# A table of task order for one Trainium2 core, rewritten up to the second chunk's first gate product

## The chip, the core and the metric

The kernel runs on one core of one Trainium2 chip. The time is the device time of one execution in microseconds. Three runs of the kernel before gave 203.19, 204.13 and 204.41 us, median 204.13 us. A run is called faster or slower than another here when they differ by more than a measurement of this kernel can tell from no change, about 1%.

## What is computed

A transformer block on x of 2048 tokens by 512, in bf16, with six modulation vectors worked out from a condition c. Its first half is a linear attention whose feature map has two softmaxes per head (32 heads of 16); its second half is a gated feed-forward of 1376 columns.

```python
mod = (silu(c) @ w_mod)                       # sa, ca, ga, sb, cb, gb
h = layernorm(x) * (1 + ca) + sa
q, k, v = split(h @ wqkv)
phi_q = concat(softmax(q @ w_phi), softmax(-(q @ w_phi)))
phi_k = concat(softmax(k @ w_phi), softmax(-(k @ w_phi)))
kv = sum over tokens of phi_k (x) v;  z = sum over tokens of phi_k
o = (phi_q @ kv) / (phi_q @ z + 1e-6)
x = x + ga * (o @ wo)
h = layernorm(x) * (1 + cb) + sb
x = x + gb * ((sigmoid(h @ w_gate) * (h @ w_up)) @ w_down)
```

## The kernel before

The 2048 tokens are 16 tiles of 128. All weights stay in SBUF. The kernel has two halves with a barrier between them, since kv needs every token's key: the keys and values of all 16 tiles first, then numerators, output product, second normalisation and feed-forward by chunks of 1, 1, 2, 4, 4 and 4 tiles (`CHUNKS`).

Each piece of work is a task with a name, a tuple of engines that can do it, and the data that it reads and writes. The names used below, with N a tile or group number:

- `ld_...`: a load, issued on SP. `warm0`, `warm1_N`: matmuls on zeros. `tpw`, `wTc`, `fold`, `foldc`: the key (1) and query (0) weights are transposed and multiplied with w_phi once, on PE, and copied out of PSUM on ACT.
- `modc1.0`, `modc1.1`, `modc1c0`, `modc1c1`: the first scale and shift, two halves, on PE and then ACT or DVE.
- `st1`, `rs1`, `nmr1`, `xn1`, `tph` or `xT1`, `hm1`: the first normalisation (statistics on DVE L702 and L703, root on ACT or POOL, mean times root on DVE L718, the normalised tile on ACT, POOL or DVE), its transposition on PE (L744) or by DMA, and the modulation into h1T (L751 on ACT, L753 on DVE and POOL).
- `K`, `e`, `n`, `r`, `phi`: key product (PE L817), two exponentials (ACT L776), their sums (DVE L780), reciprocals (DVE L798, or ACT L794 and L795) and the map (POOL or DVE L787). `V` and `va`: value product (PE L821) and its copy (ACT L836). `kv`: the sum over tokens in PSUM (PE L282); `kvn`, `kvz`: its masked copy kvb (DVE L294, L299).
- `Q`, `qe`, `qn`, `qphi`, `pT`: the same for queries (PE L871, ACT L776, DVE L780, POOL or DVE L784, two halves), and the map's transposition by DMA (SP L874).
- `num`, `rd`, `u`, `oT`, `out`: numerators (PE L326), reciprocal (DVE L329), quotient o (DVE L333), its transposition on PE or by DMA (SP L350), output product a_ps (PE L356).
- `x1`, `st2`, `rs2`, `nmr2`, `xn2`, `xnT`, `mod`: first residual sum (DVE L361), statistics, nmr (DVE L383), xn (ACT L400), transposition on PE (L415) or by DMA, modulation.
- `gK.F`, `tg`, `uK.F`, `hm`, `y`, `fin`: gate and up products of chunk K (PE L447), tanh (ACT L457), their product (DVE L468), down product (PE L485), last sum. `wo`, `wd`: the output and down weights times ga and gb (POOL L851, L860).

The order of all 1230 tasks is written out as one text, `ORDER`: one word per task, with a letter behind an @ where it isn't the task's first engine. Every engine works through its own tasks strictly in that order. `arrange` also hands out the buffers by it: a buffer's slot goes to the next task that needs one of its class once the last user stands in the list, so the order decides which earlier task a later one has to wait for. There are 8 PSUM banks, 7 buffers for maps and exponentials, and 10 for transposed query maps.

```python
for word in text.split():
    name, _, e = word.partition("@")
    t = self.tasks[name]
    t.eng = LETTER[e] if e else next(iter(t.alts))
    for b in t.bufs:
        if b.slot is None:
            b.slot = slots[b.cls].pop(0)
```

Of the kernel before, what the change touches and what calls it, by code (L numbers as in the profile page):

```python
# [43 lines left out]
hm1_00@A tph02 hm1_23 rs1_6@P hm1_13@A hm1_02 nmr1_3 st1_9 st1_8 xn1_5 tph03 K0a tph41 hm1_03@A tph40 xn1_4 K2a hm1_22@A hm1_12@A hm1_41@A hm1_40 wqT1 nmr1_6
ld_x3a st1_15 fold01 foldc01 tph42 K2b hm1_42@A K0b K3b e0.0 ld_wv0 tph32 tph30 tph31 wqT3 tph33 rs1_5@P nmr1_5 K1a hm1_32 xn1_11 hm1_30@A st1_14 n0.0 st1_12
xn1_10 xn1_9 K1b e2.0 e3.0 rs1_8@P V0a wqT2 xn1_8 hm1_31@A tph43 V2a V2b nmr1_8 xn1_15 xn1_14 ld_wmga wqT0 V3a V3b va3 V0b fold03 V1a modca.0 modca.1 hm1_33
tph50 V1b e1.0 K5a n2.0 r0.0@A modcac hm1_50 n3.0 hm1_43@A foldc03 xT1_11 fold02 fold00 foldc02 phi0.0 tph52 foldc00 xT1_10 va2 va1 n1.0 va0 K5b K4a r3.0
st1_13 tph53 hm1_63@P hm1_60@P K4b hm1_62@P Q0 hm1_53@A tph51 Q1 ld_wmm2 tph82 hm1_51@A r2.0@A Q2 r1.0 phi3.0@D phi1.0@D hm1_82@A qe0.0 Q4 modc2.0 phi2.0@D
rs1_7@P nmr1_7 xn1_12 hm1_52 qe2.0 ld_wo xn1_13 kv0.0 kv1.0 kv2.0 tph83 kv3.0 qe1.0 qn0.0 xT1_12 e5.0 modc2.1 xT1_13 modc2c K6a K6b qphi0.0@P e4.0 qn2.0
qphi0.1@P tph80 qn1.0 pT0 hm1_80@A qphi2.1 qphi2.0 pT2 K7a K7b qe4.0 n4.0 V6 va6 r4.0@A n5.0 V5 va5 tph81 V4 qn4.0 phi4.0@D qphi1.1@P r5.0@A va4 qphi1.0@P  # L50
hm1_70@P K9 K8 hm1_61@P qphi4.0@P kv4.0 pT1 phi5.0 hm1_72@P qphi4.1 e6.0 hm1_83 hm1_81 V9 n6.0 V7 pT4 hm1_71 e9.0 e7.0 va7 K11 n9.0 e8.0 e11.6 e11.0 r6.0
r9.0@A ld_wd2 n7.0 kv5.0 r7.0@A e11.2 gwa K14 V8 e14.0 phi6.0 e14.4 e11.4 n8.0 n11.6 phi7.0@D n11.0 K10 n14.0 n11.2 r8.0 r11.0 va9 kv6.0 hm1_73@P e10.0 gra
va8 K12 phi9.0 kv7.0 K15 n11.4 r11.2 V10 phi8.0 V11 n14.4 r14.0 r11.6 gwb e12.0 va10 K13 kv8.0 phi11.6 kv9.0 Q6 ld_wd r11.4 n10.0 r14.4@A wmod_free V14 V13
phi11.4@D va11 n12.0 r10.0@A phi11.0@D phi11.2@D e13.4 phi10.0@D e13.0 e15.4 kv10.0 e15.0 kv11.4 kv11.6 ld_wu0 kv11.0 kv11.2 n13.4 va13 grb V12 Q3 wo1 phi14.0
r12.0@A phi14.4 V15 qe6.0 va12 n13.0 r13.4 phi13.4 n15.0 r13.0 n15.4 r15.4@A phi15.4 r15.0 va14 phi13.0@D phi15.0@D Q5 phi12.0@D ld_wg0 kv12.0 kv13.0 va15
kv14.0 qn6.0 wo0 wo3 kv15.0 kvz0 kvn0 kv13.4 kv14.4 kv15.4 kvz1 kvn1 num0a num1a num2a wo2 rd0a wo_all rd1a qe3.0 u0a num0b num4a num1b rd0b Q11 qe5.0 rd2a
u0b u2a rd4a num2b qn3.0 u1a rd1b tpo0 Q8 qphi6.0@P qphi6.1@P oT0 out0 num4b rd2b u1b wd0 qe11.0 u2b qphi3.1@P qphi3.0@P x1_0 rd4b st2_0 qe8.0 Q7 qe7.0 tpo1
oT1 Q10 Q9 out1 Q15 oT2 rs2_0 qn5.0 nmr2_0 xn2_0 u4a u4b x1_1 qn7.0 tsw xnT0 out2 qphi5.1@P qphi5.0@P pT6 mod02 mod00 qphi7.0@P pT3 mod03@A mod01@A qe15.0
qphi7.1@P Q13 g0.8 x1_2 tg0.8 g0.1 st2_1 wd1 rs2_1 tg0.1 u0.8 u0.1 g0.0 num3b g0.4 hm0.1 hm0.8 pT5 qe9.0 tg0.4 g0.9 wd2 u0.4 u0.9 rd3b u3b tg0.9 g0.5 num3a
# [999 lines left out]
```

## Time and profile before

| what | value |
|---|---|
| runs | 203.19, 204.13, 204.41 us |
| the profiled execution's own time | 203.25 us |
| its span, first to last instruction | 201.3 us |
| PE busy | 193.6 us (96%) |
| DVE busy | 160.0 us (79%) |
| ACT busy | 104.9 us (52%) |
| POOL busy | 103.9 us (52%) |
| first gate product of the second chunk starts | 76.63 us |

An engine's row in a timeline gives its start in the span, its length, the line, what it writes and reads, and how many such instructions it holds; in brackets stands the idle time of the engine ahead of it and what ended it. PE's matmuls overlap, so a row's length is more than the time to the next start. A row for SP is the time that SP took to issue a DMA, not its transfer.

### The profile page before, as it was taken

To read this page: it belongs to the slowest core of one execution; us is meant where nothing else is said; L and a number is where in the kernel's file an instruction comes from. 1 tells how busy PE (TensorE), PEld (TensorE's weight loads), DVE (VectorE), ACT (ScalarE), POOL (GpSimd) and SP (SyncE) were. 2 spreads that over 40 slices of the span, in tenths; PEclk is the share of its full clock that TensorE was granted. 3 is DMA by queue.
4 is the path that set the end of the run, shared out by engine and by line. 5 is a ranking of instruction groups with operands and counts; after the bars stand their busy time and mean duration, and the time that the engine had idled before them with its cause. 6 is when DMAs were issued, how large, how long until landed. Compare 5 with 4: busy or idle time off the path is not lost.

```text
span 201.3 us, 4128 instructions
## 1 busy us (share of the span) xinstructions
PE 193.6 (96%) x1447; PEld 106.1 (53%) x1471; DVE 160.0 (79%) x376; ACT 104.9 (52%) x250; POOL 103.9 (52%) x146
## 2 busy tenths in 40 slices
PE   7889999999999999999999999999999999999993
PEld 2555665455565777668744444444444444444442
DVE  3999999999999999997997796875969662326632
ACT  2899999999978974486621215312112420334100
POOL 4889978887899998876660166130030332000000
PEclk9999999999999999999999999999999999999999
DMA  5999956729964883455573334442113031000011
GB/s 163 336 292 236 295 204 126 113 62 268 396 248 78 133 111 68 85 34 105 104 80 80 70 62 102 84 110 56 25 25 74 2 78 55 26 8 26 28 55 55
DMA packets 49453, 22.94 MB, mean 114 GB/s; under 512 B 38065, under 2 KB 47634, under 8 KB 49426
## 3 DMA queue, kind: packets, MB, share of 16 engines
q1 hardware_dynamic: 48896, 22.59, 48.8%
q8 instruction: 13, 0.21, 0.4%
q14 instruction: 14, 0.11, 0.2%
q10 hardware_dynamic: 530, 0.02, 0.1%
HBM read 11.58 MB, written 2.10 MB: 68 GB/s over the span
## 4 chain that ended last, share of the span: by engine, by line
PE 64%; DVE 26%; issue 5%; ACT 2%; DMA 1%; DVEq 0%
PE y_ps L485 19%; PE u_ps L447 18%; PE g_ps L447 18%; DVE ks L780 6%; PE a_ps L356 5%; DVE st L702 5%; DVE qks L780 3%; DVE phi L787 3%; DVE kr L798 2%; PE num L326 2%; DVE h1T L753 2%; DMA x_sb<-in_A_x_dram 1%; DVE mv L703 1%; PE g_ps L449 1%; DVE nmr L718 1%
## 5 line engine op out<-in xcount | busy, mean ns | idle before, releaser
L457 ACT ACTIVATE tg<-g_ps 128x512 bf16<-128x512 f32 (+5 forms) x66 | 28.7, 455 | 66.6 <-PE g_ps L447 39.7
L468 DVE SCALAR_TENSOR_TENSOR wmod_sb<-tg,u_ps 128x512 bf16<-128x512 bf16 (+4 forms) x63 | 30.2, 491 | 18.1 <-ACT tg L457 11.5
L485 PE MATMUL y_ps<-wd_sb,wmod_sb 128*128 128x512 bf16 (+4 forms) x180 | 44.2, 366 | 0.2
L447 PEld LDWEIGHTS <-wg_sb 128*128 128x128 bf16 (+1 forms) x252 | 21.9, 99 | 16.1 <-issue 0.2
L447 PEld LDWEIGHTS <-wu_sb 128*128 128x128 bf16 (+1 forms) x252 | 21.7, 99 | 15.9 <-issue 0.2
L784 POOL TENSOR_TENSOR qphi<-qe,qks 128x512 bf16<-128x512 bf16 x24 | 25.2, 1066 | 3.9 <-DMA pT<-qphi 1.6
L485 PEld LDWEIGHTS <-wmod_sb 128*128 128x128 bf16 (+1 forms) x187 | 17.1, 98 | 16.0 <-issue 0.6
L447 PE MATMUL u_ps<-wT_sb,wu_sb 128*128 128x512 bf16 (+2 forms) x124 | 23.8, 322 | 0.1
L447 PE MATMUL g_ps<-wT_sb,wg_sb 128*128 128x512 bf16 (+2 forms) x122 | 23.0, 321 | 0.2
L447 PE MATMUL g_ps<-wqk_sb,wg_sb 128*128 128x128 bf16 (+4 forms) x127 | 19.9, 286 | 0.1
L447 PE MATMUL u_ps<-wqk_sb,wu_sb 128*128 128x128 bf16 (+4 forms) x127 | 19.8, 286 | 0.1
L492 DVE TENSOR_TENSOR ot<-y_ps,x 128x512 bf16<-128x512 f32 (+2 forms) x17 | 11.1, 654 | 10.4 <-PE y_ps L485 10.3
L780 DVE TENSOR_REDUCE ks<-e 128x64 f32<-128x1024 bf16 (+2 forms) x22 | 19.2, 901 | 0.0
L780 DVE TENSOR_REDUCE qks<-qe 128x64 bf16<-128x1024 bf16 x16 | 19.1, 1202 | 0.0
L376 POOL TENSOR_SCALAR ve<-mv 128x2 f32<-128x2 f32 (+1 forms) x8 | 1.8, 225 | 33.3 <-DVE mv L366 33.2
L776 ACT ACTIVATE e<-k_ps 128x512 bf16<-128x512 f32 (+2 forms) x44 | 18.2, 519 | 0.0
L776 ACT ACTIVATE qe<-q_ps 128x512 bf16<-128x512 f32 x32 | 17.0, 611 | 0.8 <-POOL phi L787 0.5
L817 PE MATMUL k_ps<-wqk_f,h1T 128*128 128x512 bf16 x61 | 16.0, 379 | 0.1
L787 POOL TENSOR_TENSOR phi<-e,kr 128x1024 bf16<-128x1024 bf16 (+2 forms) x10 | 14.8, 1484 | 2.6 <-DVE phi L787 1.2
L356 PE MATMUL a_ps<-wo_sb,oT 128*128 128x512 bf16 x60 | 15.9, 379 | 0.2
L871 PE MATMUL q_ps<-wqk_f,h1T 128*128 128x512 bf16 x61 | 15.7, 379 | 0.1
L821 PE MATMUL v_ps<-wv_sb,h1T 128*128 128x512 bf16 x61 | 15.4, 379 | 0.1
(132 smaller groups left out, 305.6 us busy)
## 6 DMA issues: line engine op xcount, KB each, us to landing
out_dram<-ot SPq DMA_DIRECT2D x15, 128.0 KB, 1.7
x_sb<-in_A_x_dram SPq DMA_DIRECT2D x6, 256.0 KB, 4.7
wmod_sb<-in_w_mod_dram SPq DMA_DIRECT2D x1, 1536.0 KB, 7.0
wu_sb<-in_B_w_up_dram SPq DMA_DIRECT2D x1, 1376.0 KB, 11.5
wg_sb<-in_B_w_gate_dram SPq DMA_DIRECT2D x1, 1376.0 KB, 11.9
wd_sb<-in_B_w_down_dram SPq DMA_DIRECT2D x1, 1280.0 KB, 8.5
wmod_sb<-in_w_mod_dram SPq DMA_DIRECT2D x4, 256.0 KB, 6.1
wqk_sb<-in_A_wqkv_dram SPq DMA_DIRECT2D x2, 256.0 KB, 4.4
```

What stands on the lines that cost most here:

```text
L356: pe.matmul(ap_[:], lhsT=oT[:, j, :], rhs=wo_sb[:, j, :], start=(j == 0), stop=(j == KT - 1))
L447: pe.matmul(ps[:fsz, 0:n], lhsT=w[:, j, ft * P:ft * P + fsz], rhs=h[:, j, 0:n], start=(j == 0), stop=(j == KT - 1))
L457: G.add(f"tg{k}.{ft}", {"ACT": 0.13 + n * 0.00083}, lambda e, tg=tg, g_ps=g_ps, fsz=fsz, n=n: act.activation(tg[:fsz, 0:n], g_ps[:fsz, 0:n ...
L468: dve.scalar_tensor_tensor(hm_all[:fsz, hm[k].slot, ft, 0:n], tg[:fsz, 0:n], 1.0, u_ps[:fsz, 0:n], op0=ALU.add, op1=ALU.mult)
L485: mm = pe.matmul(y[:, 0:c1 - c0], lhsT=hm_all[:fsz, hm[k].slot, ft, tl * P:(tl + 1) * P], rhs=wd_sb[:fsz, ft, c0:c1], start=(ft == 0), sto ...
L776: act.activation(ee[:, a:b, s].rearrange("p g f h -> p g (f h)"), kp[:, a * 64:b * 64].rearrange("p (g n) -> p g n", n=64), ACT.Exp, scale ...
L780: dve.tensor_reduce(ks[:, a:b].rearrange("p g s h -> p (g s) h"), ee[:, a:b].rearrange("p g s f h -> p (g s) h f"), axis=AX.X, op=ALU.add)
L784: engine(e).tensor_tensor(ph[:].rearrange("p (g s f h) -> p g s f h", s=2, f=DH, h=4)[:, :, s], ee[:, :, s], ks[:, :, 1 - s].unsqueeze(2). ...
L787: engine(e).tensor_tensor(ph[:, a * P:b * P].rearrange("p (g f h) -> p g f h", f=DH, h=4), ee[:, a:b].rearrange("p g s f h -> p (g s) f h" ...
L817: pe.matmul(kp[:], lhsT=h1T[:, j, t * P:(t + 1) * P], rhs=wqk_f[:, j, D:2 * D], start=(j == 0), stop=(j == KT - 1))
L821: pe.matmul(vp[:], lhsT=h1T[:, j, t * P:(t + 1) * P], rhs=wv_sb[:, j, :], start=(j == 0), stop=(j == KT - 1))
L871: pe.matmul(qp[:], lhsT=h1T[:, j, t * P:(t + 1) * P], rhs=wqk_f[:, j, 0:D], start=(j == 0), stop=(j == KT - 1))
```

## The change

Only `ORDER` is changed, and of it only the first 581 words, up to the first gate product of the second chunk (`g1.2`); the same 1230 tasks are there, and from `g1.2` on word for word the same. Ten tasks get another engine: `xn1_3` goes from ACT to POOL and `xn1_2` from POOL to ACT; `hm1_10` from DVE to ACT and `hm1_01` from ACT to DVE; the reciprocals `r6.0` and `r14.0` from DVE to ACT, `r5.0` and `r14.4` from ACT to DVE; `qphi2.1` from DVE to POOL; `mod11` from ACT to DVE. The order of the loads on SP, and of the transpositions, is unchanged. Two lines of the table:

```diff
-wdz warm0 c1 warm1_0 warm1_1 warm1_2 warm1_3 warm1_4 warm1_5 warm1_6 warm1_7 ld_x0b pmem ld_x0a ld_wk0 tpw1 tpw0 bd c2 mask4 st1_3 st1_2 st1_1 ld_x1b warm1_8
...
+wdz warm0 c1 warm1_0 warm1_1 warm1_2 warm1_3 ld_x0b pmem mask4 ld_x0a st1_2 st1_3 rs1_2 ld_wk0 c2 st1_1 rs1_1 ld_x1b ld_wk1 bd warm1_4 nmr1_2 xn1_2@A tpw1
...
```

What it does to the engines' lists is shown at four places. On DVE, behind the first three query sums (qks), stands the query map half that changes engine; - is before, + is the change:

```order
 L780 TENSOR_REDUCE qks<-qe 128x64 x3
-L784 TENSOR_TENSOR qphi<-qe,qks 128x8x64 x2
-L780 TENSOR_REDUCE ks<-e 128x64 x2
-L780 TENSOR_REDUCE qks<-qe 128x64
+L784 TENSOR_TENSOR qphi<-qe,qks 128x8x64
+L780 TENSOR_REDUCE ks<-e 128x64
+L780 TENSOR_REDUCE qks<-qe 128x64
+L780 TENSOR_REDUCE ks<-e 128x64
 L787 TENSOR_TENSOR phi<-e,kr 128x1024
```

One of two map halves is gone from DVE's list, and a query sum goes between two key sums.

On DVE, from the masked kv (kvb, ahead of these rows) to the first tile's residual sum x and its statistics, before:

```order
L329 RECIPROCAL den<-num 128x16 x2
L333 TENSOR_TENSOR o<-num,den 128x256
L329 RECIPROCAL den<-num 128x16 x2
L333 TENSOR_TENSOR o<-num,den 128x256 x2
L329 RECIPROCAL den<-num 128x16
L780 TENSOR_REDUCE qks<-qe 128x64
L333 TENSOR_TENSOR o<-num,den 128x256
L329 RECIPROCAL den<-num 128x16 x2
L333 TENSOR_TENSOR o<-num,den 128x256 x2
L361 TENSOR_TENSOR x_1280<-a_ps,x_sb 128x512
L329 RECIPROCAL den<-num 128x16
L365 BN_STATS st_85<-x_1280 128x6
```

And in the changed kernel, the same place:

```order
L329 RECIPROCAL den<-num 128x16 x2
L333 TENSOR_TENSOR o<-num,den 128x256
L329 RECIPROCAL den<-num 128x16 x2
L333 TENSOR_TENSOR o<-num,den 128x256 x3
L329 RECIPROCAL den<-num 128x16 x2
L333 TENSOR_TENSOR o<-num,den 128x256
L780 TENSOR_REDUCE qks<-qe 128x64
L361 TENSOR_TENSOR x_1271<-a_ps,x_sb 128x512
L333 TENSOR_TENSOR o<-num,den 128x256
L365 BN_STATS st_85<-x_1271 128x6
```

Ahead of x stand six reciprocals and five quotients, seven and six before: one of each has moved behind x, and the query sum now stands last ahead of it.

On POOL, behind the last key maps (phi) and the output weights (wo_sb), stand the query maps and the down weights (wd_sb):

```order
 L787 TENSOR_TENSOR phi<-e,kr 128x512 x4
 L851 TENSOR_TENSOR wo_sb<-wo_sb,ga_sb 128x512 x3
-L784 TENSOR_TENSOR qphi<-qe,qks 128x8x64 x2
-L860 TENSOR_TENSOR wd_sb<-wd_sb,wmod_sb 128x512
-L784 TENSOR_TENSOR qphi<-qe,qks 128x8x64 x6
-L860 TENSOR_TENSOR wd_sb<-wd_sb,wmod_sb 128x512
+L784 TENSOR_TENSOR qphi<-qe,qks 128x8x64 x8
+L860 TENSOR_TENSOR wd_sb<-wd_sb,wmod_sb 128x512 x2
 L376 TENSOR_SCALAR ve_87<-mv_86 128x1
 L377 TENSOR_TENSOR rs_88<-ve_87,mhalf 128x1
```

The eight map halves of tiles 6, 3, 5 and 7 are now in one piece, and the down weight that stood between them comes behind.

On PE, the last of tile 7's numerator (pT is its transposed query map) and what follows it, before:

```order
L326 LDWEIGHTS pT_1524
L326 MATMUL num<-kvb,pT_1524 128x68
L485 LDWEIGHTS wmod_sb
L485 MATMUL y_ps<-wd_sb,wmod_sb 128x512
L356 LDWEIGHTS oT
L356 MATMUL a_ps<-wo_sb,oT 128x512
```

In the changed kernel:

```order
L326 LDWEIGHTS pT_1430
L326 MATMUL num<-kvb,pT_1430 128x68
L485 LDWEIGHTS wmod_sb
L485 MATMUL y_ps<-wd_sb,wmod_sb 128x512
L485 LDWEIGHTS wmod_sb
L485 MATMUL y_ps<-wd_sb,wmod_sb 128x512
L415 LDWEIGHTS xn_1588
L415 MATMUL tp_x<-ident,xn_1588 128x128
```

Before, the transposition of xn (L415) and one output product group (L356, four matmuls) stood ahead of the numerator; now they, and one y product, follow it.

More of the change, by code (lines that the diff above doesn't have):

```diff
@@ L44 @@
[L44 to L59, printed above, removed]
@@ new lines @@
+nmr1_7 hm1_52 e4.0 qe2.0 hm1_61@P xn1_12 xT1_12 kv0.0 kv1.0 qe1.0 hm1_51@A qn0.0 kv2.0 qn2.0 xn1_13 qphi0.0@P va6 qphi0.1@P kv3.0 Q4 V4 qn1.0 qe4.0 xT1_13
+tph81 va4 modc2.0 pT0 e5.0 modc2.1 tph80 qphi2.1@P qphi2.0 n4.0 V5 r4.0@A modc2c va5 qn4.0 V7 n5.0 phi4.0@D hm1_80@A wmod_free K7a va7 pT2 r5.0 hm1_81
+qphi1.1@P qphi1.0@P hm1_70@P tph83 hm1_83 K7b K9 kv4.0 qphi4.1 V9 hm1_71 K8 qphi4.0@P phi5.0 e6.0 e7.0 e9.0 n6.0 pT1 pT4 r6.0@A e8.0 K11 e11.4 hm1_73@P n7.0
+r7.0@A e11.6 n9.0 kv5.0 r9.0@A e11.0 K10 e11.2 K14 va9 e14.4 n8.0 ld_wd2 phi6.0 e14.0 gwa hm1_72@P n11.4 V8 va8 phi7.0@D r11.4 n11.0 n11.2 kv6.0 n11.6 K12
@@ new lines @@
+r8.0 e10.0 n14.4 n14.0 phi9.0 r11.6 kv7.0 r11.0 V10 r14.4 e12.0 K15 V13 r11.2 phi8.0 va13 r14.0@A n10.0 phi11.4@D n12.0 phi11.6 phi11.2@D r10.0@A K13 kv8.0
+kv9.0 gra e13.4 gwb V11 phi10.0@D e13.0 phi11.0@D V15 wo1 Q6 n13.4 va10 va11 phi14.4 phi14.0 e15.0 e15.4 r12.0@A n13.0 r13.4 phi13.4 kv10.0 kv11.4 kv11.6
+kv11.0 kv11.2 V14 n15.0 r13.0 V12 n15.4 r15.0 qe6.0 Q5 phi12.0@D va12 r15.4@A phi15.4 va14 phi13.0@D ld_wd phi15.0@D Q3 kv12.0 kv13.4 kv13.0 qn6.0 wo2 va15
+wo3 kv14.0 kv15.0 kvz0 kvn0 ld_wu0 kv14.4 kv15.4 kvz1 num0a kvn1 num1a num4a qe5.0 rd0a grb num2a wo0 num0b num2b qe3.0 num1b rd1a u0a rd0b rd2a u0b wo_all
@@ new lines @@
+u2a Q11 tpo0 u1a rd2b qphi6.0@P Q8 oT0 rd1b out0 qe8.0 u2b qn3.0 num4b x1_0 Q7 Q10 ld_wg0 qphi6.1@P u1b qe11.0 oT2 tpo1 qphi3.1@P qe7.0 qphi3.0@P Q9 pT6 Q15
+st2_0 rs2_0 qn5.0 nmr2_0 qphi5.0@P oT1 qphi5.1@P xn2_0 rd4b qn7.0 pT3 tsw u4b out1 rd4a xnT0 qphi7.1@P x1_1 mod02 mod03@A mod01@A mod00 out2 qphi7.0@P u4a
+x1_2 Q13 wd2 qe15.0 g0.1 pT5 st2_1 g0.8 wd0 rs2_1 u0.8 oT4 tg0.1 u0.1 num3b num3a tg0.8 hm0.8 wd1 g0.4 hm0.1 qe9.0 pT7 tg0.4 rd3b g0.9 u0.4 rd3a g0.0 tg0.9
+g0.2 u0.9 u3b wd3 u3a hm0.4 qe10.0 u0.0 hm0.9 tg0.0 num6a g0.5 wd6 rd6a num6b u0.3 hm0.0 u0.5 g0.3 rd6b tg0.2 u0.2 tg0.5 u6a hm0.5 g0.6 u6b wd4 tg0.3 hm0.2
```

16 lines of the change are left out of this document (10 added, 6 removed).

## The prediction

> **What bounds the kernel now.** I read the page first, then the busy time by stretches, cut where the work changes character: the start up to the first key product, the keys and values up to the end of their sum, the first chunk's part that is still reordered, and what nobody touches.
>
> ```profile
> span 201.3 us, 4128 instructions
> PE y_ps L485 19%; PE u_ps L447 18%; PE g_ps L447 18%; DVE ks L780 6%; PE a_ps L356 5%; DVE st L702 5%; DVE qks L780 3%; DVE phi L787 3%; DVE kr L798 2%; PE num L326 2%; DVE h1T L753 2%; DMA x_sb<-in_A_x_dram 1%; DVE mv L703 1%; PE g_ps L449 1%; DVE nmr L718 1%
> ```
>
> ```profile
> core 0: us, PE busy (x) PEld busy (x) DVE busy (x) ACT busy (x) POOL busy (x), PEclk, DMA share, GB/s
> 0.00:13.00 13.00, 10.61 (x101) 5.57 (x102) 9.58 (x31) 8.74 (x21) 8.97 (x31) 1.00 0.93 254
> 13.00:56.40 43.40, 42.62 (x397) 23.90 (x401) 43.08 (x91) 42.35 (x116) 37.91 (x43) 1.00 0.85 223
> 56.40:76.60 20.20, 19.88 (x217) 13.26 (x220) 19.71 (x60) 17.05 (x42) 19.96 (x21) 1.00 0.67 127
> 76.60:197.80 121.20, 120.46 (x740) 63.37 (x752) 87.32 (x197) 36.71 (x74) 37.10 (x54) 1.00 0.30 59
> ```
>
> The chain shares its time between PE and DVE; the table says why. Between 13.0 and 56.4 us three engines are full at once: PE lacks 43.40 - 42.62 = 0.78 us, DVE 0.32 us, ACT 1.05 us. From 56.4 to 76.6 us PE lacks 0.32 us, and from there to its last matmul at 197.8 us another 0.74 us in 121.2 us. So PE is the floor: whatever the order, the same matmuls have to go through it after 13.0 us.
>
> Is a full PE really paced by its own work? The spacing answers that.
>
> ```profile
> 40.08 0.43 PE L282 MATMUL kvacc<-vaug,phi 128*128 128x68 bf16 x8 [0.20 <-POOL phi L787]
> ...
> 43.20 1.02 PE L817 MATMUL k_ps<-wqk_f,h1T 128*128 128x512 bf16 x4
> 44.06 0.42 PE L282 MATMUL kvacc<-vaug,phi 128*128 128x68 bf16 x8
> ```
>
> Four products of 512 columns start at 43.20 and the next group at 44.06, 0.86 us later, 0.216 each. Each single one is shown as 1.02 - 3 x 0.216 = 0.37 us long, so a gap shorter than about 0.16 us doesn't show as idle; allowing for that, PE's real gaps between 13.0 and 76.6 us are an estimated 1.1 to 1.7 us. That is all there is to win there. [...] The even 0.216 us starts decide here for the floor.
>
> **The change part by part.** The sum is made against the profiled execution: 203.25 us, of which the span is 201.3. The median of the three runs is 204.13 us, 0.88 above it; I put the sum's difference on the median.
>
> *What is not moved.* From the second chunk's first gate product on (the row at 76.63 below), every engine has the list it had. PE is full there, so the end moves by what that product moves, and no more than that unless another engine falls behind. The loads stand in the same order on SP.
>
> ```profile
> 1.25 2.74 PE L600 MATMUL warm<-wd_sb 128*128 128x512 bf16 x6 [1.25 <-DVE wd_sb L593]
> ...
> 4.11 2.15 PE L600 MATMUL warm<-wd_sb 128*128 128x512 bf16 x8
> 6.09 0.61 PE L661 MATMUL tp_w<-ident,wqk_sb 128*128 128x128 bf16 x8
> ...
> 12.58 0.55 PE L630 MATMUL modc_ps<-sc_bf,wmod_sb 128*128 128x1 bf16 x16 [0.46 <-DMA wmod_sb<-in_w_mod_dram]
> 12.99 0.38 PE L817 MATMUL k_ps<-wqk_f,h1T 128*128 128x512 bf16 x1
> ```
>
> *The start, 0 to 13 us.* The first key product stands right behind the scale's matmuls, and these waited for a load (0.46 us at 12.58). In the changed list the same load comes as the eleventh on SP as before, and nearly the same matmuls go ahead of the key product (0.05 us of transpositions more). So this point stays: 0, up to +0.1 because banks come free later:
>
> ```profile
> 9.17 1.59 ACT L685 CAST wqk_f<-fold_ps 128x512 bf16<-128x512 f32 x3
> ...
> 10.72 0.18 ACT L636 ACTIVATE modc<-modc_ps 128x2 f32<-128x2 f32 x1
> ...
> 11.12 0.34 DVE L753 TENSOR_SCALAR h1T<-tp_h,modc 128x128 bf16<-128x128 bf16 x1
> 11.38 0.32 DVE L718 TENSOR_SCALAR nmr<-mv,rs 128x1 f32<-128x1 f32 x2
> 11.62 0.68 DVE L702 BATCH_NORM_STATS2 st<-x_sb 128x6 f32<-128x512 bf16 x1
> ```
>
> ACT now copies all four folded key blocks ahead of the scale, three before; one copy takes (10.67 - 9.17) / 3 = 0.50 us with 10.67 as the scale's start, just ahead of the row at 10.72. So the scale ends at 10.90 + 0.50 = 11.40. DVE has one nmr pair more ahead of its first h1T (11.62 - 11.38 = 0.24) and gets there at 11.36; with the 0.06 to 0.1 us from an engine's end to the next one's start it waits some 0.13 us. DVE is full, so that is +0.13 for DVE.
>
> *DVE up to the end of the key sum.* The pairs that change engine cancel (one xn from ACT to POOL and one back; one h1T of 128x128, one reciprocal of 64 and one of 32 columns each way between ACT and DVE). What doesn't cancel is one query map half, which goes from DVE to POOL.
>
> ```profile
> 32.05 0.75 DVE L784 TENSOR_TENSOR qphi<-qe,qks 128x512 bf16<-128x512 bf16 x2
> 32.72 2.33 DVE L780 TENSOR_REDUCE ks<-e 128x64 f32<-128x1024 bf16 x2
> ...
> 56.42 0.41 DVE L294 TENSOR_TENSOR kvb<-kvacc,mask 128x256 bf16<-128x256 f32 x1
> ...
> 58.38 0.25 DVE L329 RECIPROCAL den<-num 128x16 f32<-128x16 f32 x1
> 58.55 1.16 DVE L780 TENSOR_REDUCE qks<-qe 128x64 bf16<-128x1024 bf16 x1
> ```
>
> Two halves take 32.72 - 32.05 = 0.67 us, so one is -0.33. POOL pays a little over 1.0 us for it (2.06 for two, below); it idles 43.40 - 37.91 = 5.49 us in this stretch, which hides it; without that cover its later maps would come 1.0 us late. The last kvb, and with it the first numerator on PE, so moves by -0.33 + 0.13 = -0.20 us. PE must be there too: its own gaps ahead of that point are 0.78 us and more, which covers -0.20. Were the cover gone, two or three new waits of PE as long as the one at 40.08 (0.20) would make it +0.5: between 13 and 25 us transpositions now stand where they wait for a bank that ACT has only just left.
>
> *From the numerators to the first gate product.* One reciprocal (58.55 - 58.38 = 0.17) and one numerator product (0.30) now stand behind the first x1 on DVE instead of ahead of it. That brings x1 and its statistics another -0.47 nearer. PE doesn't gain it: it is full from here, so the gate products move with PE's -0.20 and the -0.47 is slack for the chain through ACT.
>
> *POOL's down weights.* One wd scaling stood between query maps and now stands behind all of them.
>
> ```profile
> 59.12 2.06 POOL L784 TENSOR_TENSOR qphi<-qe,qks 128x512 bf16<-128x512 bf16 x2
> 61.15 1.15 POOL L860 TENSOR_TENSOR wd_sb<-wd_sb,wmod_sb 128x512 bf16<-128x512 bf16 x1
> 62.27 6.37 POOL L784 TENSOR_TENSOR qphi<-qe,qks 128x512 bf16<-128x512 bf16 x6
> ...
> 62.26 5.50 SPq L874 DMA_TRANSPOSE pT<-qphi  x3
> 67.93 1.19 SPq L350 DMA_TRANSPOSE oT<-o  x1
> 69.22 1.93 SPq L874 DMA_TRANSPOSE pT<-qphi  x1
> ...
> DMA to landing us min/median/max: 3.0/3.3/4.7
> ...
> 71.90 0.59 PE L485 MATMUL y_ps<-wd_sb,wmod_sb 128*128 128x512 bf16 x2
> ```
>
> The six maps start 62.27 - 61.15 = 1.12 us sooner, so the transpositions on SP behind them can too: the one of 69.22 goes to about 68.1. The landing line is that of all sixteen map transpositions. The first y product, which needs that wd, comes at 71.90 - 0.2 = 71.7 us; the maps end at 68.64 - 1.12 = 67.5 and two scalings by 69.8. Hidden by 1.9 us.
>
> *The numerator of tile 7, the tight place.* PE had it at 74.56. Ahead of it stood four output products (0.86), a transposition (0.22) and a y product (0.22) that now stand behind it.
>
> ```profile
> 71.04 0.12 DVE L383 TENSOR_SCALAR nmr<-mv,rs 128x1 f32<-128x1 f32 x1
> ...
> 71.86 0.81 ACT L400 ACTIVATE xn<-x,nmr,rs 128x512 bf16<-128x512 f32 x1
> ...
> 73.03 1.03 PE L356 MATMUL a_ps<-wo_sb,oT 128*128 128x512 bf16 x3
> ...
> 74.34 0.39 PE L415 MATMUL tp_x<-ident,xn 128*128 128x128 bf16 x4
> 74.56 0.29 PE L326 MATMUL num<-kvb,pT 128*128 128x68 bf16 x4
> ...
> 76.63 0.61 PE L447 MATMUL g_ps<-wT_sb,wg_sb 128*128 128x128 bf16 x8
> ```
>
> So it is due at 74.56 - 1.30 - 0.20 = 73.06. Its transposition, issued near 68.1, lands at 68.1 + 3.3 = 71.4, or 72.8 by the worst of the sixteen: in time by 0.26 at the least. The transposition of xn2 (74.34) now stands 0.52 earlier on PE, due 74.34 - 0.52 - 0.20 = 73.62, while its nmr stands behind two reciprocals (0.17), three numerator products (0.33) and two gate products (0.2) more, less what DVE gained: 71.04 + 1.73 - 0.33 = 72.4. ACT's xn of 0.81 then ends at 73.3: in time by 0.3. One modulation of the second chunk goes from ACT to DVE, behind an x1 that follows the output products: these end at 73.62 + 0.22 + 1.03 = 74.87, x1 and the modulation add about 0.6 and 0.3, 75.8, and PE wants it at 76.4. What waits behind either on PE is everything up to the second chunk. Cost 0, with both ends kept.
>
> *Sum*: 0 (start) - 0.20 (DVE's kvb) + 0 (numerators) + 0 (second chunk) = -0.2 us: 203.05 for the profiled execution, 203.9 for the median. Bounds: -1.1 to -1.7 if every PE gap closes; +0.5 from the slots, +0.7 to +1.5 from the tight place.
>
> **The rivals.** *PE stops at the tight place.* If the map transposition takes as long as the slowest row from the old issue time, it lands at 69.22 + 4.7 = 73.92 and PE stands 0.86 us; with -0.20 that is +0.66, 204.8. It decides as soon as POOL's 1.12 us don't reach SP, or a landing is over 4.96 us. A second late one (tile 5's, due some 2 us earlier) would add as much: 205.6 at the far end. For it: all of SP's transpositions there queue behind one another. Against: the wd move.
>
> *Small waits add up early.* Between 13 and 25 us every engine but POOL is full, and the banks are handed on at once; +0.5 on DVE instead of -0.2: 204.6.
>
> *All gaps close.* DVE meets no new wait and PE uses the whole 1.1 us that the table shows: 203.0; with the hidden part 202.4.
>
> *The clock.* In 1.25 to 3.99 us six warm products take 2.74 us, 0.43 apart, and from 4.5 us on 0.216: PE starts at half speed. Three of the eight warm products at 4.11 now run later, and PE is idle 3 x 0.216 = 0.65 us ahead of the weights at 6.09. If full speed came later by the 3.2 us that it took here, products from 13 us on could run at half speed for up to 3.2 us: +1.6, 205.7. Against it: PE stood idle 0.46 us at 12.58 and the products after it kept their 0.216. [...]
>
> *The change does nothing*: PE's floor holds both, 204.1; it can't be told from the forecast.
>
> **How the numbers follow.** A measurement of this kernel can tell about 1%, 2.0 us, from no change. The forecast with the no-effect case has 0.62; PE stopping 0.15; early waits 0.10; all gaps closed 0.08; the clock 0.04; 0.01 for what I don't see. Faster by over 1% needs more than the 1.7 us that PE has: only a scatter of the runs (203.19 to 204.41) on top of the all-gaps case gets there, 0.04. Slower by over 1% means above 206.2: the far ends of PE stopping, of early waits and of the clock together, 0.10. Within 1%: 0.86. The range 202.8 to 205.4 leaves out the far ends on both sides, about 1 in 10 each.
>
> **What would show it.** Right: the first key product at 12.9 to 13.1; the last kvb on DVE 0.1 to 0.4 sooner than 56.42; POOL's query maps of tiles 3, 5 and 7 in one piece from about 61.2; no idle mark at the numerator group behind the gate products near 73; the row of the second chunk's first gate product near 76.4; the same PE busy time in the last stretch. Wrong: an idle mark with a DMA or the nmr as its releaser between 70 and 75 us (PE stopped), h1T or tp_h rows with waits that push kvb past 56.6 (early waits), products 0.43 apart beyond 6 us (the clock), or a gate product more than 1.7 us sooner, which would say that PE wasn't the floor.

## The result and the profile after

The changed kernel takes 204.52 us (median of 19 runs, 204.23 to 206.18), the kernel before in the same session 203.52 us (19 runs, 202.86 to 205.93). The ratio is 1.0053, with a 95% interval of 1.0029 to 1.0076: about 1.1 us slower, inside the 1% that was called no change, but on the other side of the forecast of -0.2. The profiled execution took 204.52 us with a span of 202.6, against 203.25 and 201.3: +1.27.

In these two traces the last matmul starts 1.65 us later (199.24 against 197.59). What follows it, the last sums and the stores, took 3.33 us in the changed kernel and 3.72 before, which gives back 0.39 and leaves 1.27. That last stretch has the same list in both kernels, and in the traces of all the runs here it takes 3.30 to 3.81 us. So it is the 1.65 that has to be explained.

The busy times by stretches, changed kernel:

```profile
core 0: us, PE busy (x) PEld busy (x) DVE busy (x) ACT busy (x) POOL busy (x), PEclk, DMA share, GB/s
0.00:13.00 13.00, 11.23 (x97) 6.15 (x98) 9.49 (x31) 8.56 (x21) 9.57 (x31) 1.00 0.94 254
13.00:56.40 43.40, 42.70 (x394) 23.82 (x398) 43.13 (x87) 42.41 (x115) 37.61 (x44) 1.00 0.84 213
56.40:76.60 20.20, 19.60 (x226) 13.26 (x226) 19.36 (x60) 16.37 (x39) 19.64 (x20) 1.00 0.64 141
```

This table alone would say that nothing has happened up to 56.4 us: PE is busy 42.70 us there (42.62 before), DVE 43.13 (43.08). Only the instruction counts hint at it: DVE got through 87 instructions instead of 91, PE through 394 matmuls instead of 397. The marks along PE's timeline show where the time went. Changed kernel, PE: the first key product, the last part of the key sum, the first numerator, the numerator of tile 7, the first gate product of chunk 1:

```profile
13.17 0.38 PE L817 MATMUL k_ps<-wqk_f,h1T 128*128 128x512 bf16 x1
...
55.61 1.18 PE L282 MATMUL kvacc<-vaug,phi 128*128 128x68 bf16 x32
...
57.23 1.05 PE L326 MATMUL num<-kvb,pT 128*128 128x68 bf16 x28 [0.44 <-DVE kvb L294]
...
74.16 0.29 PE L326 MATMUL num<-kvb,pT 128*128 128x68 bf16 x4
...
78.29 0.61 PE L447 MATMUL g_ps<-wT_sb,wg_sb 128*128 128x128 bf16 x8 [0.59 <-ACT wT_sb L426]
```

Against the kernel before: first key product 13.17 (12.99), first numerator 57.23 (56.47), chunk 1's gate product 78.29 (76.63). The 0.18 of the start isn't carried: see below. Two pieces make up the rest. DVE's last kvb (the masked key sum, which the numerators wait for) starts at 57.08 instead of 56.42, +0.66. And from there to chunk 1's gate product it takes 78.29 - 57.08 = 21.21 us instead of 76.63 - 56.42 = 20.21, +1.00, with a new stop of PE at its end. The first numerator of the kernel before:

```profile
56.47 0.97 PE L326 MATMUL num<-kvb,pT 128*128 128x68 bf16 x24 [0.33 <-DVE kvb L294]
```

Where DVE lost its 0.66, first in DVE's rows with query maps (qphi), one key map (phi) and the last kvb, changed kernel:

```profile
32.28 1.29 DVE L784 TENSOR_TENSOR qphi<-qe,qks 128x512 bf16<-128x512 bf16 x1
...
36.88 0.68 DVE L787 TENSOR_TENSOR phi<-e,kr 128x1024 bf16<-128x1024 bf16 x1
...
38.49 0.55 DVE L784 TENSOR_TENSOR qphi<-qe,qks 128x512 bf16<-128x512 bf16 x1
...
57.08 0.42 DVE L294 TENSOR_TENSOR kvb<-kvacc,mask 128x256 bf16<-128x256 f32 x1
```

and POOL's query maps of the same time:

```profile
30.21 3.08 POOL L784 TENSOR_TENSOR qphi<-qe,qks 128x512 bf16<-128x512 bf16 x3
33.74 2.07 POOL L784 TENSOR_TENSOR qphi<-qe,qks 128x512 bf16<-128x512 bf16 x2 [0.45 <-DVE qphi L784]
```

The one map half that DVE kept took 1.29 us. It started at 32.28, POOL's third half ran from about 32.23 to 33.29, and DVE's ended at 33.57, 0.28 us behind POOL's. The half that went to POOL for DVE's sake stood in the way of the half that stayed. The kernel before had the same thing once, the other way round, and it was there to be read:

```profile
36.81 0.42 DVE L784 TENSOR_TENSOR qphi<-qe,qks 128x512 bf16<-128x512 bf16 x1
...
36.88 1.27 POOL L784 TENSOR_TENSOR qphi<-qe,qks 128x512 bf16<-128x512 bf16 x1 [0.79 <-DVE phi L787]
```

DVE was there first by 0.07 us and took its usual 0.42; POOL's half took 1.27 instead of 1.05. So an instruction that is held, that is, kept from going on by the other engine's, doesn't show as idle here: it is shown as busy, and longer, POOL's by 0.22 us at this place and DVE's by 0.88 at 32.28. Up to here this is a reading of rows; the experiments below test it. POOL's half of 32.23 started 0.05 us ahead, and DVE's took 1.29 us and ended 0.28 behind it. What was held are maps, both of whose inputs lie in SBUF. Key and query sums, with one input, kept their 1.2 us beside POOL's maps (1.20 at 34.62, beside POOL's of 33.74 to 35.81), and so did the residual sum x, which has one of its two inputs in PSUM, its 0.68 (at 61.22, beside POOL's maps of 59.72 to 63.82; 0.68 to 0.69 where POOL did nothing).

The stop at chunk 1, changed kernel, ACT's modulations (wT_sb) of that chunk and DVE's rows around its own:

```profile
75.47 0.47 ACT L426 ACTIVATE wT_sb<-tp_x,modc 128x128 bf16<-128x128 bf16 x1
77.43 0.81 ACT L426 ACTIVATE wT_sb<-tp_x,modc 128x128 bf16<-128x128 bf16 x2 [1.49 <-DVE wT_sb L422]
```

```profile
76.21 0.67 DVE L361 TENSOR_TENSOR x<-a_ps,x_sb 128x512 f32<-128x512 f32 x1
76.81 0.27 DVE L468 SCALAR_TENSOR_TENSOR wmod_sb<-tg,u_ps 128x128 bf16<-128x128 bf16 x1
77.00 0.33 DVE L422 TENSOR_SCALAR wT_sb<-tp_x,modc 128x128 bf16<-128x128 bf16 x1
```

ACT did `mod12`, then stood for 1.49 us until DVE's `mod11` was done, and only then did `mod13` and `mod10`. Both `mod11` and `mod13` read `tps[1]` (line 420, `tps[j % 2]`), one PSUM bank, and in this trace, where they are on two engines, the later reader waits for the earlier one: `mod11` ends at 77.33 and ACT goes on at 77.43. In chunk 0, where DVE has one bank and ACT the other, the two engines work side by side (ACT's two modulations from 66.44, DVE's two from 66.47) and nobody waits. Why two readers of one bank follow each other no run here shows; what is seen is the wait, 1.49 us.

### The profile page after: what moved, and what is told of

Same layout as the page of the kernel before. It is cut to its first block, busy times and chain, and to the rows that moved or that the text cites. A ratio compares the mean times of both kernels' runs of the same rounds, so it can differ in the third digit from the quotient of the medians.

```text
span 202.6 us, 4135 instructions
## 1 busy us (share of the span) xinstructions
PE 195.1 (96%) x1447; PEld 107.0 (53%) x1471; DVE 161.2 (80%) x376; ACT 104.9 (52%) x249; POOL 104.7 (52%) x147
## 4 chain that ended last, share of the span: by engine, by line
PE 81%; DVE 8%; ACT 4%; issue 2%; DMA 1%; POOL 1%; DVEq 0%; POOLq 0%; ACTq 0%
PE y_ps L485 18%; PE g_ps L447 18%; PE u_ps L447 18%; PE q_ps L871 5%; PE a_ps L356 5%; PE k_ps L817 5%; PE v_ps L821 4%; PE num L326 2%; DVE ks L780 2%; DVE phi L787 1%; DMA x_sb<-in_A_x_dram 1%; PE g_ps L449 1%; DVE qks L780 1%; PE kvacc L282 1%; ACT h1T L751 1%
## 5 line engine op out<-in xcount | busy, mean ns | idle before, releaser
L485 PE MATMUL y_ps<-wd_sb,wmod_sb 128*128 128x512 bf16 (+3 forms) x179 | 44.0, 366 | 0.3
L784 POOL TENSOR_TENSOR qphi<-qe,qks 128x512 bf16<-128x512 bf16 x25 | 25.9, 1057 | 4.1 <-DVE phi L787 1.3
L817 PE MATMUL k_ps<-wqk_f,h1T 128*128 128x512 bf16 x62 | 16.5, 378 | 0.1
L787 POOL TENSOR_TENSOR phi<-e,kr 128x1024 bf16<-128x1024 bf16 (+2 forms) x10 | 14.6, 1472 | 2.4 <-DVE phi L787 1.8
L356 PE MATMUL a_ps<-wo_sb,oT 128*128 128x512 bf16 x61 | 15.6, 379 | 0.1
```

Source lines behind the costliest of these rows:

```text
L356: pe.matmul(ap_[:], lhsT=oT[:, j, :], rhs=wo_sb[:, j, :], start=(j == 0), stop=(j == KT - 1))
L485: mm = pe.matmul(y[:, 0:c1 - c0], lhsT=hm_all[:fsz, hm[k].slot, ft, tl * P:(tl + 1) * P], rhs=wd_sb[:fsz, ft, c0:c1], start=(ft == 0), sto ...
L784: engine(e).tensor_tensor(ph[:].rearrange("p (g s f h) -> p g s f h", s=2, f=DH, h=4)[:, :, s], ee[:, :, s], ks[:, :, 1 - s].unsqueeze(2). ...
L787: engine(e).tensor_tensor(ph[:, a * P:b * P].rearrange("p (g f h) -> p g f h", f=DH, h=4), ee[:, a:b].rearrange("p g s f h -> p (g s) f h" ...
L817: pe.matmul(kp[:], lhsT=h1T[:, j, t * P:(t + 1) * P], rhs=wqk_f[:, j, D:2 * D], start=(j == 0), stop=(j == KT - 1))
```

## The experiments

In what follows a hold is what a map instruction on DVE (L784, L787) took beyond the usual length of its shape, 0.41 us for 512 columns, 0.68 for 1024, 0.28 for 256, added up to the first kvb. Counted so, the kernel before has 0.17 us of holds (the expectations say 0.27, which took in a later map behind kvb), the changed kernel 1.07.

The ratios given are to the kernel before, timed beside the run. In these sessions that kernel had medians of 204.6 to 205.0 us, where it had 203.52 above, and the 95% intervals are 0.5 to 0.9% wide. So the ratios decide none of the questions, and the argument goes by the traces, one of each kernel.

**The map half back on DVE.**

```diff
-qphi2.1@P qphi2.0 n4.0
+qphi2.1 qphi2.0 n4.0
```

> The changed kernel with the map half qphi2.1 given back to DVE, right ahead of qphi2.0, as it was before. In the changed kernel DVE's one half (L784 at 32.28 us) took 1.29 us while POOL worked on the other half (32.23 to 33.29), where before a half took 0.33 to 0.41. Theory A (DVE's half is held until POOL's half is through): the pair takes 0.75 on DVE as before, DVE's last kvb comes 1.29 - 0.75 = 0.54 us sooner, near 56.5, and the time falls by 0.3 to 0.5 us, to about 204.1. Theory B (my prediction's step: moving the half saved DVE 0.33 us, and the loss is from waits in the start): kvb comes 0.33 us later, near 57.4, and the time rises by 0.3, to about 204.8.

The ratio is 1.0030 (0.9992 to 1.0068), the profiled execution 205.08 us, where theory A had about 204.1. Locally theory A held: the pair took 0.75, and DVE's next key map started at 36.27 instead of 36.88. But kvb came at 57.82, later than in the changed kernel. DVE's and POOL's key maps (phi) and the output weights (wo_sb) further on in this run:

```profile
49.48 1.67 DVE L787 TENSOR_TENSOR phi<-e,kr 128x256 bf16<-128x256 bf16 x3
...
54.11 2.16 DVE L787 TENSOR_TENSOR phi<-e,kr 128x1024 bf16<-128x1024 bf16 x3
```

```profile
49.02 1.17 POOL L851 TENSOR_TENSOR wo_sb<-wo_sb,ga_sb 128x512 bf16<-128x512 bf16 x1 [0.80 <-DMA ga_sb<-gdr]
51.02 3.18 POOL L787 TENSOR_TENSOR phi<-e,kr 128x512 bf16<-128x512 bf16 x3 [0.83 <-DVE phi L787]
54.89 1.10 POOL L787 TENSOR_TENSOR phi<-e,kr 128x512 bf16<-128x512 bf16 x1 [0.69 <-ACT kr L795]
```

The same two groups on DVE took 1.13 and 1.31 us in the changed kernel. DVE, 0.6 us earlier, now ran into POOL's wo scaling (its first map held 0.59), and its last map began at 55.01, 0.12 behind POOL's, and was held 0.85. The gain of 0.6 was made, and more than lost a few us later. The scaling works on other data than the map, so it isn't the shared tile that holds DVE.

**The same work, DVE's half one place later.**

```diff
-qphi2.1@P qphi2.0 n4.0
+qphi2.1@P n4.0 qphi2.0
```

> The changed kernel with two words exchanged: DVE's map half qphi2.0 behind the key sum n4.0 instead of ahead of it. Every engine keeps its work; only these two change places on DVE. Theory A (held by POOL's half): POOL's half ends near 33.3 while DVE sums, so the half at 33.4 takes 0.41 us instead of 1.29; kvb comes up to 0.88 us sooner (56.2 to 56.6), the first numerator too as far as PE allows, and the time falls by 0.4 to 0.8 us, to 203.7 to 204.1. Theory B (DVE's half is long for a reason of its own, or PE is late from the start's waits anyway): the half stays long, or kvb moves by under 0.2 us, and the time stays within 0.2 of 204.5.

1.0043 (1.0006 to 1.0081), profiled 205.85 us. DVE's half, and POOL's three that end ahead of it at 33.49:

```profile
33.63 0.41 DVE L784 TENSOR_TENSOR qphi<-qe,qks 128x512 bf16<-128x512 bf16 x1
```

```profile
30.40 3.09 POOL L784 TENSOR_TENSOR qphi<-qe,qks 128x512 bf16<-128x512 bf16 x3
```

The half took 0.41 us, as theory A says and B doesn't; yet kvb came at 58.45, because three later maps were held by 0.24, 0.82 and 0.85. The mechanism was right, the time I gave for it wrong: I had priced one hold and left the others where they were.

**The modulations ahead.**

```diff
-x1_4 hm0.7 qphi11.0@P qphi11.1@P out3 mod11 x1_3 st2_3 oT6 mod13@A mod10@A
+mod13@A mod10@A x1_4 hm0.7 qphi11.0@P qphi11.1@P out3 mod11 x1_3 st2_3 oT6
```

> The changed kernel with the words mod13 and mod10 ahead of x1_4, and so ahead of mod11. ACT and DVE keep their lists; only who waits changes: ACT's mod13 no longer waits for DVE's mod11 (1.49 us at 77.43), DVE's mod11 waits for mod13 instead, which is then long done. Theory C (the stop of PE at the second chunk's first gate product, 0.75 us, comes from this wait): that product starts 0.6 to 0.75 us sooner, near 77.6, with no idle mark, and the time falls by 0.6 to 0.75, to about 203.8. Theory D (the product waits because PE's own earlier work, and with it the transposition of xn2, is late): it moves by under 0.2 us and the time stays at 204.3 to 204.5.

1.0016 (0.9981 to 1.0051), profiled 204.69 us. This run's ACT and PE at the place:

```profile
75.56 1.17 ACT L426 ACTIVATE wT_sb<-tp_x,modc 128x128 bf16<-128x128 bf16 x3
```

```profile
74.60 0.30 PE L326 MATMUL num<-kvb,pT 128*128 128x68 bf16 x4 [0.18 <-ACT xn L400]
...
75.39 2.75 PE L356 MATMUL a_ps<-wo_sb,oT 128*128 128x512 bf16 x12
```

ACT does its three modulations in one piece, and the gate product, at 77.98, follows the output products without a stop. It came only 0.31 sooner, since a new stop of 0.34 us stood ahead of tile 7's numerator at 74.60. The stop is read from the starts: eight products of 0.056 us from 73.81 end at 74.26, where the row's bracket, which goes by modelled ends, has 0.18. The releaser that is named there had been done; it was the transposed map. What the trace says of that one DMA (issued at 69.2 us), in this run and then in the changed kernel:

```profile
L874 SPq DMA_TRANSPOSE pT<-qphi x1: 2268/2268/2268, 69.2 to 69.2; - x1
...
DMA to landing us min/median/max: 5.4/5.4/5.4
```

```profile
L874 SPq DMA_TRANSPOSE pT<-qphi x1: 2239/2239/2239, 69.1 to 69.1; - x1
...
DMA to landing us min/median/max: 3.6/3.6/3.6
```

5.4 us against 3.6 with the same list on SP: it landed at 74.6, and PE wanted it at 74.26. From kvb to the gate product this run took 20.80 us; less the 0.34 it is 20.46, 0.75 under the changed kernel's 21.21. Theory C, and the size it gave for the wait, hold. The time of about 203.8 didn't come: the profiled execution was 0.17 over the changed kernel's, since the gate product won only 0.31 and what follows the last matmul took 3.81 us instead of 3.33.

**Both at once.**

```diff
-qphi2.1@P qphi2.0 n4.0
+qphi2.1@P n4.0 qphi2.0
...
-x1_4 hm0.7 qphi11.0@P qphi11.1@P out3 mod11 x1_3 st2_3 oT6 mod13@A mod10@A
+mod13@A mod10@A x1_4 hm0.7 qphi11.0@P qphi11.1@P out3 mod11 x1_3 st2_3 oT6
```

> Both edits at once: qphi2.0 behind n4.0, and mod13 and mod10 ahead of x1_4. If theories A and C hold and the two losses lie one behind the other on PE, they add: the gate product of the second chunk comes 1.1 to 1.6 us sooner than in the changed kernel (76.7 to 77.2), and the time is 203.0 to 203.4, at or just below the kernel before, which is about what the prediction's sum gave without the two losses. If they cover the same slack, the time is that of the better one alone, 203.7 to 203.9. If the start's waits hold PE (theory B), at most 203.8.

1.0021 (0.9993 to 1.0048), profiled 204.99 us, where 203.0 to 203.4 was expected. From kvb to the gate product 20.45 us, so the second loss is gone; kvb at 58.33 with 2.21 us of holds, so the first has grown. DVE's two groups of key maps:

```profile
49.63 2.05 DVE L787 TENSOR_TENSOR phi<-e,kr 128x256 bf16<-128x256 bf16 x3
...
54.64 2.14 DVE L787 TENSOR_TENSOR phi<-e,kr 128x1024 bf16<-128x1024 bf16 x3
```

```profile
49.95 1.57 POOL L851 TENSOR_TENSOR wo_sb<-wo_sb,ga_sb 128x512 bf16<-128x512 bf16 x1 [1.58 <-DMA ga_sb<-gdr]
```

POOL's scaling, in the second fence, waited for its load until 49.95 here, and DVE's third map of the first group was held 0.97 behind it; the last map of the second group 0.85, behind POOL's map of 55.41.

**One part alone: the half to POOL, in the kernel before.**

```diff
-qphi2.1 qphi2.0 pT2
+qphi2.1@P qphi2.0 pT2
```

> The kernel before with one of the ten engine changes alone: the query map half qphi2.1 goes from DVE to POOL; every other word stays. The sum of my prediction gave -0.33 us on DVE for this: kvb 0.33 us sooner, near 56.1, and the time unchanged or 0.3 lower. Theory A (a DVE instruction with two inputs in SBUF and a POOL instruction cannot run at once; DVE is held until POOL's is through): the other half on DVE takes about 1.29 instead of 0.41, kvb comes later, not sooner. With kvb = 56.15 (kernel before, less the 0.27 us by which its halves and maps on DVE were held) - 0.33 + the sum of the holds of this run, it is 56.8 to 57.8, and the time 0.4 to 1.4 us above the kernel before.

> The kernel before with qphi2.1 on POOL once more, for a look at an execution in which TensorE is at full speed from the first key product on (in the one profiled it was not). Theory A: kvb = 56.15 - 0.33 + the sum of the holds on DVE, within 0.2; the holds again more than in the kernel before (0.27), so kvb is above 56.1. By the prediction's step kvb is 56.1 and no DVE instruction is longer than in the kernel before.

Ratio 1.0024 (0.9986 to 1.0063). In both profiled executions of this kernel TensorE fell back to half speed from 13.9 to 17.3 us (a granted clock of 0.50 and 0.51), so their times (207.18 and 207.09 us) and positions aren't compared; the lengths can be. DVE's maps in the second of them:

```profile
34.19 0.41 DVE L784 TENSOR_TENSOR qphi<-qe,qks 128x512 bf16<-128x512 bf16 x1
...
38.34 0.93 DVE L787 TENSOR_TENSOR phi<-e,kr 128x1024 bf16<-128x1024 bf16 x1
...
39.19 1.27 DVE L784 TENSOR_TENSOR qphi<-qe,qks 128x512 bf16<-128x512 bf16 x1
...
56.69 2.25 DVE L787 TENSOR_TENSOR phi<-e,kr 128x512 bf16<-128x512 bf16 x3
```

Half a miss. I expected tile 2's half to take 1.29; here DVE came to it 0.01 us ahead of POOL and took 0.41. But POOL was then late: its modulation (L753, 38.18 to 38.73) held DVE at 38.34 (by 0.25), its next half, from 38.85 on, at 39.19 (0.86); the last map was held once more, 0.85. In all 2.10 us of holds instead of 0.17 (2.08 in the other execution). The step that my sum had at -0.33 brings holds of some 1.9 us with it. How much of that reaches the end can't be read from these two; the timed ratio allows anything from 0.3 us won to 1.3 us lost.

**The other part alone: mod11 to DVE, in the kernel before.**

```diff
-mod13@A mod12@A rd7a x1_4 y0.3 out3 qphi11.1@P qphi11.0@P x1_3 st2_3 out6 mod10@A mod11@A
+mod12@A rd7a x1_4 y0.3 out3 qphi11.1@P qphi11.0@P mod11@D x1_3 st2_3 out6 mod13@A mod10@A
```

> The kernel before with another engine change alone: mod11 goes from ACT to DVE, behind x1_4 and ahead of x1_3, with mod13 and mod10 behind it in the list as in the changed kernel. Nothing differs ahead of 74 us. Theory C (ACT's mod13 reads the PSUM bank that mod11 reads and so waits for it): mod11 runs on DVE at about 76.0 to 76.35, ACT's mod13 and mod10 follow to 77.2, and the second chunk's first gate product starts near 77.3 instead of 76.63; the time is 0.6 to 0.7 above the kernel before. By my prediction's step (mod11 hidden on DVE by 0.6 us) it stays at 76.6 and the time doesn't change.

```profile
77.43 0.61 PE L447 MATMUL g_ps<-wT_sb,wg_sb 128*128 128x128 bf16 x8 [0.36 <-ACT wT_sb L426]
```

```profile
76.57 0.81 ACT L426 ACTIVATE wT_sb<-tp_x,modc 128x128 bf16<-128x128 bf16 x2 [1.13 <-DVE wT_sb L422]
```

These rows are PE's and ACT's. ACT waits 1.13 us for DVE, and the gate product comes 20.85 us behind kvb instead of 20.21: +0.64, as expected. The profiled execution took 203.86 us, 0.61 over that of the kernel before; the timed ratio, 1.0022 (0.9978 to 1.0066), agrees but could not tell it from nothing.

**One cause taken away: POOL's scaling at 50 us, of which the kernel does 8 columns and leaves out 504.**

```diff
-        G.add(f"wo{j}", {"POOL": 1.1, "DVE": 0.62}, port=("POOL", "DVE"), fn= lambda e, j=j: engine(e).tensor_tensor(wo_sb[:, j, :], wo_sb[:, j, :], ga_sb[:], op=ALU.mult),
+        G.add(f"wo{j}", {"POOL": 1.1, "DVE": 0.62}, port=("POOL", "DVE"), fn= lambda e, j=j, w=(8 if j == 1 else D): engine(e).tensor_tensor(wo_sb[:, j, 0:w], wo_sb[:, j, 0:w], ga_sb[:, 0:w], op=ALU.mult),
```

> The kernel of the two edits at once (qphi2.0 behind n4.0, mods ahead) with POOL's scaling of the second output weight block cut from 512 columns to 8, so that this block stays unscaled; nothing else differs. In that kernel DVE's map instruction at 50.43 us was held 0.97 us behind this scaling, which works on other data. Theory A: that hold is gone, DVE runs up to 0.97 us sooner from there, and kvb, at 58.33, comes 0.7 to 1.0 sooner, unless the next map on DVE is held in its place; in any case kvb = 56.0 + the sum of the holds, within 0.2. If DVE's long instructions were not due to POOL, kvb stays within 0.2 of 58.33.

DVE's two groups of key maps, the last kvb, and POOL's scaling and last key map:

```profile
49.60 1.08 DVE L787 TENSOR_TENSOR phi<-e,kr 128x256 bf16<-128x256 bf16 x3
...
53.65 1.31 DVE L787 TENSOR_TENSOR phi<-e,kr 128x1024 bf16<-128x1024 bf16 x3
...
56.61 0.42 DVE L294 TENSOR_TENSOR kvb<-kvacc,mask 128x256 bf16<-128x256 f32 x1
```

```profile
49.51 0.20 POOL L851 TENSOR_TENSOR wo_sb<-wo_sb,ga_sb 128x8 bf16<-128x8 bf16 x1 [1.17 <-DMA ga_sb<-gdr]
...
54.73 1.14 POOL L787 TENSOR_TENSOR phi<-e,kr 128x512 bf16<-128x512 bf16 x1 [0.98 <-ACT kr L795]
```

Both holds are gone, the one at the scaling and, since DVE now came to its last map 0.18 us ahead of POOL, that one too; 0.40 us of holds are left. kvb comes at 56.61, 1.72 us sooner than with both edits and the full scaling, and the one profiled execution took 203.23 us. Of everything that POOL does, a piece of 1.2 us on other data was enough to move DVE by 1.7. Chunk 1's gate product came at 77.06, still 0.43 behind the kernel before.

**Both halves on POOL, and the modulations ahead.**

```diff
-qphi2.1@P qphi2.0 n4.0
+qphi2.1@P qphi2.0@P n4.0
...
-x1_4 hm0.7 qphi11.0@P qphi11.1@P out3 mod11 x1_3 st2_3 oT6 mod13@A mod10@A
+mod13@A mod10@A x1_4 hm0.7 qphi11.0@P qphi11.1@P out3 mod11 x1_3 st2_3 oT6
```

> The changed kernel with mod13 and mod10 ahead of x1_4, and with both map halves of tile 2 on POOL (qphi2.0 too), so that nothing of DVE is held there and DVE has 0.41 us less to do. Theory A: that hold of 0.88 is gone, and kvb = 55.9 - 0.41 + the sum of the holds that are left or new. With the holds of the changed kernel's other places (0.3) kvb would be near 55.8 and the time about 202.9; with holds of 1.5 to 2 as in the two kernels that moved a half, kvb is 57 to 57.5 and nothing is won against the changed kernel but the 0.75 of the wait at the second chunk, 203.8. If holds don't set kvb, it comes 1.29 us sooner than 57.08, whatever the holds.

1.0042 (1.0014 to 1.0069), profiled 204.89 us. From kvb to the gate product 20.45 again. kvb at 58.04, later than any of my cases. Of the 1.29 us that DVE had won, a wait for ACT took most:

```profile
32.30 1.22 DVE L780 TENSOR_REDUCE ks<-e 128x64 f32<-128x1024 bf16 x1
34.34 1.22 DVE L780 TENSOR_REDUCE qks<-qe 128x64 bf16<-128x1024 bf16 x1 [0.81 <-ACT e L776]
...
54.32 2.17 DVE L787 TENSOR_TENSOR phi<-e,kr 128x1024 bf16<-128x1024 bf16 x3
```

0.81 us there, and the last map lost to POOL's by 0.05 us and was held 0.86.

All profiled executions but the two of the half alone, with the DMA's 0.34 inside the 20.80:

| kernel | holds, us | kvb at | kvb less holds | kvb to gate product | profiled time |
|---|---|---|---|---|---|
| before | 0.17 | 56.42 | 56.25 | 20.21 | 203.25 |
| changed | 1.07 | 57.08 | 56.01 | 21.21 | 204.52 |
| half back on DVE | 1.62 | 57.82 | 56.20 | 21.20 | 205.08 |
| half later | 2.06 | 58.45 | 56.39 | 21.21 | 205.85 |
| modulations ahead | 1.22 | 57.18 | 55.96 | 20.80 | 204.69 |
| half later, modulations ahead | 2.21 | 58.33 | 56.12 | 20.45 | 204.99 |
| the same, small scaling | 0.40 | 56.61 | 56.21 | 20.45 | 203.23 |
| before, mod11 on DVE | 0.17 | 56.58 | 56.41 | 20.85 | 203.86 |
| both halves on POOL, modulations ahead | 1.49 | 58.04 | 56.55 | 20.45 | 204.89 |

kvb moves over 2.0 us, kvb less holds over 0.6; without the last row, whose extra wait for ACT is known, over 0.45. So the holds account for most of what kvb does, and not for all of it. The distance from kvb to the gate product has one value for the old list (20.21), one for the new list (21.21), and one for the new list without the wait for `mod11` (20.45). From the gate product to the last matmul all eleven traces take 120.94 to 120.96 us. The last column differs by up to 0.5 us from what the others would give, by the last sums and stores.

## Why the prediction was wrong, step by step

- *The start, 0 to +0.1.* The working held to a few hundredths: the scale began at 11.17, as the sum has it, ended at 11.47 (11.40), and DVE's first modulation began at 11.51 (11.49). From ACT's end to DVE's start that is 0.04, where the working had 0.06 to 0.1 (in the kernel before it is 0.06 from DVE's xn to PE's weight load at 11.26, and 0.09 from DVE's mv to POOL's ve at 8.61). The first key product came 0.18 later all the same (13.17). No cost of it is seen: in the modulations-ahead run the product came at 13.33, and kvb less holds at 55.96, sooner than the kernel before has it (56.25).
- *DVE up to the end of the key sum, -0.20.* This is the first of two steps that failed, in the term "one is -0.33". Without holds the change did bring kvb forward, 56.01 against 56.25, -0.24 where the sum has -0.20. What the sum left out is the price of a map instruction on one engine to the other: 1.07 - 0.17 = +0.90. The cover that was named for POOL's extra 1.0 us, its idle time, wasn't a cover, for DVE's own half, run in that time, took 1.29 us instead of 0.41. The edit was costed by the duration of a row in the kernel before, the pair at 32.05 us, and beside that row POOL stood idle from 32.09 on; POOL's 1.27 at 36.88 was the row that showed what happens otherwise.
- *"PE is the floor from 13 us."* Right behind kvb, where every shift was passed on to the last matmul (+1.66 at the gate product, +1.65 there); not ahead of it, where DVE's chain set kvb, 0.66 later, with PE's busy time at 42.70 against 42.62.
- *x1 on DVE 0.47 nearer.* Measured from kvb, the first x1 started 0.35 us sooner than before (61.22 - 57.08 = 4.14 against 60.91 - 56.42 = 4.49). It was slack, as said.
- *POOL's down weight, maps 1.12 us sooner.* Tile 7's map ended 0.25 sooner, not 1.12: POOL's maps began at 59.72 instead of 59.12, and stood 0.47 us between tiles 3 and 5 for DVE's sum (62.97 to 64.16; the releaser that the row names had long been done):

```profile
59.72 4.10 POOL L784 TENSOR_TENSOR qphi<-qe,qks 128x512 bf16<-128x512 bf16 x4
64.29 4.10 POOL L784 TENSOR_TENSOR qphi<-qe,qks 128x512 bf16<-128x512 bf16 x4 [0.47 <-POOL qphi L784]
```

  The transposition was issued at 69.1 instead of 68.1 as forecast.
- *The tight place.* No stop in the changed kernel, but for another reason than argued: PE itself came to tile 7's numerator at 74.16, 1.1 later than the 73.06 of the working, and the map had landed at 72.7. In the modulations-ahead run it did stop, 0.34 us, by the mechanism of the first rival and near its point: 5.4 us to landing, where the rival put the limit at 4.96. The working for xn2 took off 0.33 for what DVE gains, where its own sum has 0.20; the margin would have been 0.2 instead of 0.3, which changes nothing.
- *mod11 on DVE, "hidden".* The second step that failed. I set DVE's end (75.8) against PE's need (76.4) and didn't ask who else stands behind `mod11`: on ACT, two modulations that read its bank. DVE also ended later, at 77.33: the output products began 1.1 later than argued (74.94 against 73.84), and a query sum and a product for the feed-forward stood ahead. Cost 0.76 here, 0.64 alone in the kernel before. The remaining 0.24 of the second piece stays open in part: 0.10 is there at the first numerator, which starts 0.15 behind the last kvb's start instead of 0.05 (57.23 - 57.08 against 56.47 - 56.42); the other 0.14 is small gaps of PE that no run took apart.
- *The rivals.* "Small waits add up early" had the nearest time (204.6), and that is luck: it has DVE late between 13 and 25 us by banks, where DVE was late from 32 us on by maps on DVE that POOL's instructions held (1.07 us up to kvb). It also calls POOL the engine that isn't full there, and POOL was busy for 11.75 of those 12.00 us in the kernel before. "All gaps close" didn't happen. The clock: PE did reach full speed late, at 7.06 us instead of 4.65, but long before the first key product, and the scale was on time; the last section has more.

The sum gave -0.2; with +0.90 for holds, +0.76 for the modulation and +0.24 of gaps it is +1.7 at the last matmul, where 1.65 was measured; the last stretch then gave back 0.39. Not tried: an order in which the changed kernel's list keeps its full scaling without the holds. By the row with the small scaling it would end near the kernel before (203.23 against 203.25, an estimate), so no version that beats both was in sight.
